# Linear attention feeding a bilinear FFN: narrow column tiles for the first two batches, batch 1 woven into the FFN, kv by chunk

## The chip, the cores and the metric

The kernel runs on one core of one Trainium2 chip. The metric is device time in microseconds (us), the median of several executions. The time of the kernel before was 353.69 us (three runs, 353.16 to 354.46). The span in a profile is about 2 us shorter than the device time of the same run. Engines are named as in the profile: PE (matrix multiply), PEld (its weight loads), DVE (VectorE), ACT (ScalarE), POOL (GpSimd, here a DMA issuer), SP (SyncE, here the second DMA issuer).

## The reference

```python
# q, k, v: (8 batches, 8 heads, 576 tokens, 64) float32; g_norm: (64,)
kv  = np.einsum('bhsd,bhse->bhde', k, v)            # 64 x 64 per head
out = np.einsum('bhsd,bhde->bhse', q, kv)
rms = np.sqrt(np.mean(out * out, axis=-1, keepdims=True) + 1e-06)
x   = (out / rms * g_norm)                          # -> (4608 tokens, 512)
y   = ((x @ w_a) * (x @ w_b)) @ w_out               # 512 -> 1536 -> 512
```

The attention part has no softmax. A whole batch must be reduced into kv before one of its tokens can be finished.

## The kernel before

The FFN works in nine strips of 512 tokens. A strip has 12 columns `fc` (eight 512-column matmuls each, `a` and `b`), and four output groups of 12 matmuls. While strip s runs, the attention of batch s+1 is woven into it: one call of `step` after each column or group (each such place is a *slot*). Strip 0 needs batch 0, so batch 0 comes first, alone, and batch 1 runs alone between strip 0 and strip 1. These two take the "early" path: q is transposed on PE, because the DMA transposition through scratch memory would be too late (batch 2's landed only at 62.4 us).

```python
# early path, batches 0 and 1: reorder on DVE, so that two heads lie side by side (128 columns)
def early_in(self, hs):
    for n in ("k", "q"):
        nc.vector.tensor_copy(t[n + "r"][:, :, hs, :],
                              t[n][:, hs, :, :].rearrange("p h c d -> p c h d"))
def qT(self, p, ...):
    for c in range(EC):                                        # 6 chunks of 96 tokens
        nc.tensor.transpose(ps[:, c*EP:(c+1)*EP], self.t["qr"][:, c, hs, :], ident[0:EP, 0:EP])
    ... copy to qs ...
def kv(self, p, ...):                                          # both paths
    rows = [EP] * EC if self.early else [128] * NCH + [SB]     # late: 128,128,128,128,64
    for c, r in enumerate(rows):
        nc.tensor.matmul(self.kv_ps[i][:, p, :], lhsT=self.k[0:r, c, hs, :],
                         rhs=self.v[0:r, hs, c, :], start=(c == 0), stop=(c == len(rows)-1))

# per head pair p and half h of the tokens, all batches
def xu(self, p, h):   # x = kv^T q on PE;  sq = x*x on ACT
def ss(self, p, h):   # sum of squares on PE; rs = 1/sqrt on ACT; xt = x*g*rs on DVE

def slices(self):                       # the ten steps of a batch from 2 on
    for p in range(NP):                 # four pairs of heads
        self.kv(p)
    self.kv_out(0, NP); yield
    ... eight steps of xu and the ss of the half before, and a last ss ...

dummies(24)
...batch 0...; columns 0 to 11 of strip 0; dummies(4); ...batch 1, in two halves...   # cut
for s in range(1, N_STRIP):
    nxt = s + 1 if s + 1 < B else None
    if nxt:
        load_qT(loaded[nxt])            # transposing DMA on the SP queue
        ...
    o_at = [4, 6, 8, 10] if s == 1 else [2, 5, 8, 11]
    t_at, s_at = (7, 9) if s == 1 else (0, 2)      # slots: reorder of k, first step
    ...
```

`dummies(n)` are n matmuls on zeros, whose only use is to keep PE active.

## Time and profile before

| what | value | view |
|---|---|---|
| time, span | 353.69 us, 352.1 us | times, page |
| PE busy | 332.4 us (94%) | page, part 1 |
| 512-column matmul, start to start | 0.216 us; 1296 of them are 280 us | single starts in the trace |
| batch 0, to strip 0's third column | 25.65 us | timeline |
| batch 1 alone | 42.7 to 60.98 us | timeline, windows |
| strip 1 | 60.98 to 98.62 us | timeline, windows |
| kv of a later batch | 1.94 us for 20 matmuls (the prediction said 1.85, from the chain) | timeline |

The page of the kernel before. The rows of digits are 40 slices of the span, each digit a busy share in tenths; PEclk is the clock that PE was granted.

```profile
span 352.1 us, 4345 instructions
...
PE 332.4 (94%) x1643; PEld 157.9 (45%) x1674; DVE 134.7 (38%) x229; ACT 134.2 (38%) x276; POOL 59.6 (17%) x71
...
PE   8689956999989999999999999999999999999995
...
PEclk9679976999989999999999999999999999999999
...
PE 90%; DVE 3%; ACT 2%; DMA 2%; issue 2%; POOL 0%; ACTq 0%; DVEq 0%; POOLq 0%
```

PE is the bound, as the chain of waits (last line) says too. What is left to win is where the PE row is below 9 or the clock row is below 9: near the start, around slices 5 and 6, counted from 0 (batch 1), and in slice 11 (end of strip 1).

The windows view of the kernel before, for the last ten columns of strip 0, for batch 1, and for strip 1:

```profile
core 0: us, PE busy (x) PEld busy (x) DVE busy (x) ACT busy (x) POOL busy (x), PEclk, DMA share, GB/s
25.65:42.70 17.05, 17.00 (x78) 7.70 (x79) 7.50 (x11) 6.16 (x11) 10.12 (x11) 1.00 1.32 202
42.70:60.98 18.28, 11.84 (x74) 5.83 (x75) 8.64 (x16) 8.18 (x20) 9.66 (x8) 0.75 1.71 177
60.98:98.62 37.64, 36.09 (x179) 17.00 (x181) 14.10 (x23) 15.09 (x32) 6.39 (x6) 0.98 1.33 141
```

Batch 1 alone holds PE busy for 11.84 of 18.28 us, at three quarters of the clock, and partly with zeros. The timeline (start, duration, engine, line, what; in brackets the idle time before it and its releaser) shows how it begins:

```profile
42.92 1.03 PE L172 MATMUL w_ps<-zt 128*128 128x512 bf16 x4
...
43.80 1.51 DVE L220 COPY kr_t<-k_t 96x1536 bf16<-96x1536 bf16 x1
45.23 0.54 DVE L220 COPY eqr_98<-eq_97 96x1536 bf16<-96x1536 bf16 x1
...
45.82 0.68 PE L235 MATMUL q_ps<-ident,eqr_98 96*128 96x96 bf16 x12 [1.88 <-DVE eqr_98 L220]
```

Transposes wait for the two reorder copies. Then the timeline of PE for one later kv group, and for the end of strip 1:

```profile
176.01 2.01 PE L202 MATMUL kv_ps<-v_t,kr_t 128*128 128x128 bf16 x20
```

```profile
97.05 0.28 PE L258 MATMUL s_ps<-sq,ones 128*128 128x288 bf16 x1 [0.70 <-ACT rs L260]
97.60 0.28 PE L244 MATMUL x_ps<-qT,kvd_123 128*128 128x288 bf16 x1 [0.27 <-DVE xt_155 L262]
...
98.48 0.30 PE L258 MATMUL s_ps<-sq,ones 128*128 128x288 bf16 x1 [0.28 <-DVE xt_155 L262]
...
99.92 0.59 PE L307 MATMUL a_ps<-xt_156,wa_t 128*128 128x512 bf16 x1 [0.49 <-DVE xt_156 L262]
```

Seven slots were left for ten steps, so three run bare at the end of the strip. The matmul of 0.59 us in the last line already runs at half clock (0.38 at full clock).

### The profile page before, as it was taken

To read this page: it belongs to the slowest core of one execution; us is meant where nothing else is said; L and a number is where in the kernel's file an instruction comes from. 1 tells how busy PE (TensorE), PEld (TensorE's weight loads), DVE (VectorE), ACT (ScalarE), POOL (GpSimd) and SP (SyncE) were. 2 spreads that over 40 slices of the span, in tenths; PEclk is the share of its full clock that TensorE was granted. 3 is DMA by queue.
4 is the path that set the end of the run, shared out by engine and by line. 5 is a ranking of instruction groups with operands and counts; after the bars stand their busy time and mean duration, and the time that the engine had idled before them with its cause. 6 is when DMAs were issued, how large, how long until landed. Compare 5 with 4: busy or idle time off the path is not lost.

```text
span 352.1 us, 4345 instructions
## 1 busy us (share of the span) xinstructions
PE 332.4 (94%) x1643; PEld 157.9 (45%) x1674; DVE 134.7 (38%) x229; ACT 134.2 (38%) x276; POOL 59.6 (17%) x71
## 2 busy tenths in 40 slices
PE   8689956999989999999999999999999999999995
PEld 3444423445435444544454445444544444444442
DVE  2544453342442453245334533453344232332310
ACT  1543344313643643364336433643464212223211
POOL 8746527006015001500110000000000000000000
PEclk9679976999989999999999999999999999999999
DMA  7999999989939913990591040004001000011022
GB/s 106 197 196 200 206 180 167 181 78 142 150 69 136 125 32 75 151 134 30 81 171 41 30 98 31 30 33 95 33 30 30 32 31 31 30 53 39 30 61 89
DMA packets 78981, 32.14 MB, mean 91 GB/s; under 512 B 49776, under 2 KB 74352, under 8 KB 78960
## 3 DMA queue, kind: packets, MB, share of 16 engines
q0 software_dynamic: 59408, 18.88, 49.6%
q1 hardware_dynamic: 19552, 12.98, 14.3%
q8 instruction: 13, 0.21, 0.3%
q14 instruction: 8, 0.07, 0.0%
HBM read 37.75 MB, written 12.98 MB: 144 GB/s over the span
## 4 chain that ended last, share of the span: by engine, by line
PE 90%; DVE 3%; ACT 2%; DMA 2%; issue 2%; POOL 0%; ACTq 0%; DVEq 0%; POOLq 0%
PE a_ps L307 27%; PE o_ps L332 26%; PE b_ps L307 26%; PE kv_ps L202 4%; PE s_ps L258 3%; PE x_ps L244 2%; DMA v_t<-in_v_dram 2%; ACT rs L260 2%; PE q_ps L235 1%; DVE kr_t L220 1%; DVE xt_156 L262 0%; ACT sq L252 0%; DVE xt_153 L262 0%; DVE xt_155 L262 0%; DVE xt_154 L262 0%
## 5 line engine op out<-in xcount | busy, mean ns | idle before, releaser
L319 DVE TENSOR_TENSOR abt<-b_ps,a_sb 128x512 bf16<-128x512 f32 x108 | 74.6, 692 | 117.1 <-PE b_ps L307 112.5
L332 PE MATMUL o_ps<-wo_t,abt 128*128 128x512 bf16 x419 | 97.7, 379 | 0.6
L317 ACT CAST a_sb<-a_ps 128x512 bf16<-128x512 f32 x108 | 63.3, 587 | 91.1 <-PE a_ps L307 89.7
L307 PEld LDWEIGHTS <-wb_t 128*128 128x128 bf16 x432 | 42.5, 98 | 53.5 <-issue 3.8
L332 PEld LDWEIGHTS <-abt 128*128 128x128 bf16 x432 | 41.8, 98 | 48.0
L307 PEld LDWEIGHTS <-wa_t 128*128 128x128 bf16 x432 | 42.7, 99 | 45.8 <-issue 2.5
L307 PE MATMUL a_ps<-xt_156,wa_t 128*128 128x512 bf16 x108 | 41.1, 381 | 1.6 <-DVE xt_156 L262 1.6
L307 PE MATMUL b_ps<-xt_153,wb_t 128*128 128x512 bf16 x108 | 41.7, 386 | 0.2 <-issue 0.2
L307 PE MATMUL a_ps<-xt_155,wa_t 128*128 128x512 bf16 x108 | 41.2, 382 | 0.3
L307 PE MATMUL b_ps<-xt_155,wb_t 128*128 128x512 bf16 x108 | 41.2, 381 | 0.2
L307 PE MATMUL a_ps<-xt_153,wa_t 128*128 128x512 bf16 x106 | 40.9, 386 | 0.3
L307 PE MATMUL b_ps<-xt_154,wb_t 128*128 128x512 bf16 x105 | 40.0, 381 | 0.0
L307 PE MATMUL a_ps<-xt_154,wa_t 128*128 128x512 bf16 x103 | 39.5, 384 | 0.2 <-issue 0.2
L307 PE MATMUL b_ps<-xt_156,wb_t 128*128 128x512 bf16 x101 | 38.5, 381 | 0.0
L252 ACT ACTIVATE sq<-x_ps 128x288 bf16<-128x288 f32 x64 | 25.9, 411 | 31.7 <-PE x_ps L244 31.6
L260 ACT ACTIVATE rs<-s_ps,eps_t 128x288 f32<-128x288 f32 x64 | 31.9, 498 | 14.6 <-PE s_ps L258 14.2
L343 DVE COPY o_sb<-o_ps 128x512 f32<-128x512 f32 x18 | 12.4, 692 | 45.4 <-PE o_ps L332 45.4
L341 ACT COPY o_sb<-o_ps 128x512 f32<-128x512 f32 x18 | 10.6, 586 | 49.4 <-PE o_ps L332 46.5
L258 PE MATMUL s_ps<-sq,ones 128*128 128x288 bf16 x64 | 19.8, 310 | 4.3 <-ACT rs L260 1.9
L66 POOL DMA_DIRECT2D k_t<-in_k_dram x6 | 5.4, 896 | 91.7 <-DVE kr_t L179 86.7
L146 POOL DMA_DIRECT2D scr<-in_q_dram x12 | 19.6, 1640 | 6.2 <-DMA wo_t<-in_moe_w_out_dram 5.3
L202 PE MATMUL kv_ps<-v_t,kr_t 128*128 128x128 bf16 (+2 forms) x168 | 16.6, 231 | 0.3 <-DMA v_t<-in_v_dram 0.2
(68 smaller groups left out, 158.4 us busy)
## 6 DMA issues: line engine op xcount, KB each, us to landing
out_dram<-o_sb SPq DMA_DIRECT2D x24, 256.0 KB, 2.0
scr<-in_q_dram POOLq DMA_DIRECT2D x12, 288.0 KB, 12.3
k_t<-in_k_dram POOLq DMA_DIRECT2D x6, 512.0 KB, 7.5
v_t<-in_v_dram POOLq DMA_DIRECT2D x6, 512.0 KB, 8.0
wa_t<-in_moe_w_a_dram POOLq DMA_DIRECT2D x6, 256.0 KB, 9.2
wb_t<-in_moe_w_b_dram POOLq DMA_DIRECT2D x6, 256.0 KB, 10.1
wo_t<-in_moe_w_out_dram POOLq DMA_DIRECT2D x2, 768.0 KB, 14.8
out_dram<-o_sb SPq DMA_DIRECT2D x12, 128.0 KB, 2.4
```

Source lines behind the costliest of these rows:

```text
L146: nc.gpsimd.dma_start(out=scr[:, :, hl, :].rearrange("p s d -> s p d"), in_=qv[hl])
L202: nc.tensor.matmul(self.kv_ps[i][:, p, :], lhsT=self.k[0:r, c, hs, :], rhs=self.v[0:r, hs, c, :], start=(c == 0), stop=(c == len(rows) - 1),)
L244: nc.tensor.matmul(ps, lhsT=self.kvd[:, p, :], rhs=self.q[p][:, h * HF : (h + 1) * HF], start=True, stop=True,)
L252: nc.scalar.activation(sq, ps, AF.Square)
L258: nc.tensor.matmul(ps, lhsT=ones, rhs=self.sq[p, h], start=True, stop=True)
L260: nc.scalar.activation(rs, ps, AF.Abs_reciprocal_sqrt, bias=eps_t)
L307: nc.tensor.matmul(getattr(self, which), lhsT=w[:, kc, self.fc * 128 : (self.fc + 1) * 128], rhs=xt[kc][:, t0 : t0 + STRIP], start=(kc == ...
L317: nc.scalar.copy(a_sb, self.a)
L319: nc.vector.tensor_mul(t, self.b, a_sb)
L332: nc.tensor.matmul(o_ps, lhsT=ab[s, fc][:, g * 128 : (g + 1) * 128], rhs=wo_t[:, fc, :], start=(fc == 0), stop=(fc == FC - 1),)
L341: nc.scalar.copy(o_sb, o_ps)
L343: nc.vector.tensor_copy(o_sb, o_ps)
```

## The change

Its intent: drop the reorder copies by working on one head at a time (64 columns of the array each, two heads in two column tiles); load batch 0 by pair of heads with q first; weave batch 1 into the last two columns of strip 0 and into three output groups, each cut in half over its 12 matmuls; order the later kv by chunk; start batch 2 earlier in strip 1. The first 256 columns of `w_a` and `w_b` are also loaded in two pieces instead of one, and the first two columns of strip 0 are ordered anew. The core of the diff:

```diff
-        def early_in(self, hs): ...                      # the DVE reorder copies are gone
+        def early_kv(self, p, pool):
+            ps = pool.tile([128, D], FP32, name="kv_ps", tag=tags[pool])
+            for hl in range(2):
+                for c in range(EC):
+                    nc.tensor.matmul(ps[hl * D : (hl + 1) * D, :],
+                        lhsT=t["k"][:, 2 * p + hl, c, :], rhs=t["v"][:, 2 * p + hl, c, :],
+                        start=(c == 0), stop=(c == EC - 1))
+        def early_qT(self, p, pool, act=False):           # same, 12 transposes 96x64
...
+        def kv(self):                                     # batches 2 to 7
+            for c in range(NCH + 1):
+                r = 128 if c < NCH else SB
+                for p in range(NP):
+                    nc.tensor.matmul(ps[:, p, :], lhsT=self.k[0:r, c, hs, :], ...,
+                        start=(c == 0 and p == 0), stop=(c == NCH and p == NP - 1))
...
-    dummies(24)
+    dummies(22)
+    for p in range(NP):                                   # batch 0, pair by pair
+        if p == 0: at0.early_qT(0, fpsum)
+        at0.early_kv(p, fpsum)
+        ...
+        dummies(1)
+        at0.xu(p, 0); at0.xu(p, 1)
+        if p + 1 < NP: at0.early_qT(p + 1, fpsum)
+        ...
+    for fc in range(2, 10): ffn_ab(0, fc)
+    at1.early_qT(0, apsum); at1.early_qT(1, apsum, act=True)
+    ffn_ab(0, 10)
+    at1.early_kv(0, apsum); at1.early_kv(1, apsum)
+    ffn_ab(0, 11)
+    ... xu, ss, early_qT, early_kv of batch 1, with o_mm(0, g, range(0, 6)) for g = 0, 1, 2 between ...
+    for g in range(3):
+        o_mm(0, g, range(6, FC)); o_out(0, g)
...
-        o_at = [4, 6, 8, 10] if s == 1 else [2, 5, 8, 11]
-        t_at, s_at = (7, 9) if s == 1 else (0, 2)
+        o_at = {10: 3} if s == 1 else {2: 0, 5: 1, 8: 2, 11: 3}
+        t_at, s_at = (4, 5) if s == 1 else (0, 2)
...
-                        step(gen)
+                        step(gen, 2 if s == 1 and slot in (7, 10) else 1)
```

## The prediction

> **What bounds it now.** The tensor engine. The page has PE busy 332.4 of 352.1 us; the chain that ended last is 90% PE. In the timeline a 512-column matmul starts every 0.216 us when dense: 1296 FFN matmuls are a floor of 280 us. The rest:
>
> - Start to 25.6 us, batch 0. Timeline: transposes at 8.5, first x at 10.85, last xt at 24.6; the slice row shows the clock down to 0.6 around 11 to 21 us.
> - 42.7 to about 62 us, batch 1: 19 us almost without FFN work. A DVE reorder of k (1.51 us) and q, then the ACT/DVE chain per half (sq 0.41, rs 0.50, xt 0.52); windows give clock 0.76.
> - End of strip 1 (97 to 103.4 us): batch 2's last steps, not woven, leave gaps near 3 us; a half-clock window then costs about 1.7 us.
> - kv of batches 2 to 7: 1.85 us per 20 matmuls. Single starts: 0.056 us between 128-row chunks, but 0.151 into and 0.159 out of the 64-row chunk, four times a batch.
> - 3.6 us tail, unchanged.
>
> **What the change does**
>
> 1. kv by chunk: one visit to 64 rows instead of four. Three visits x 0.2 us x 6 batches: **-3.6 us**, all on PE, which is critical. The Trainium skill, "TensorEngine Tiling (Array Packing)", Key Properties, says that changing tiling mode drains the engine; the trace agrees (about 0.2 us a visit).
> 2. Batch 0: loads by pair, q first, no DVE reorder copies. First x at about 9.4 us; then about 3.1 us a pair (sq, sq, rs, rs, xt, kv copies in series), 3.5 if the clock drops; strip 0's third FFN column starts at about 23.8 instead of 25.65: **-1.8 us** (0 to -3).
>    Added: twice as many transposes and kv matmuls, each with 64 columns. "TensorE: Matmul & The Clock Gate", section LDWEIGHTS, gives columns/1.2 ns, 53 ns for 64; so I estimate 55 to 60 ns each, 0.65 to 0.7 us per 12, against 0.043 and 0.056 each before with half as many. No run shows it yet. Plus mode switches.
> 3. Batch 1 woven: from its first transpose to strip 1 there are now two FFN columns (3.45 us) and three output groups (7.8 us). PE work is about 18.3 us, with switches about 20. Exposed about 9 us instead of 19: **-10 us** (-7 to -12).
> 4. Strip 1: batch 2 starts at slot 5, with two double steps, so all ten steps end inside the strip: **-4 us**. Against it: its transposed q is now issued behind output stores on the SP queue, landing near 68 us, just when wanted: up to +1.5.
>
> Sum about -19 us. From below: strip 1 at 57.6, plus 165.7 (columns), 85.5 (33 groups), 19.7 (six batches), 3.6, and 1 of stalls = 333 us span, 335 us on the device.
>
> **Prediction: 335 us, 8 in 10 within 330 to 341.** Faster by over 2%: 0.95; within: 0.04; slower: 0.01.
>
> **Right if**: kv groups take 1.25 to 1.3 us; no gap over 1 us nor cold window at the end of strip 1; strip 1 starts at 56 to 59 us; 64-column matmuls start 50 to 60 ns apart.
>
> **Wrong if**: 64-column weight loads do not overlap the matmuls (100 ns each would add 4 us per batch); the woven section goes to half clock; batch 2's transposed q or the second half of the output weights (landing near 47 us) comes late; or batch 0 runs cold, over 4 us a pair, giving back step 2.

## The result, and the profile after

The changed kernel took 339.11 us (median of four runs: 339.70, 335.17, 339.81, 338.52) against 354.02 us of the kernel before in the same rounds. The ratio is 0.956, with a 95% interval of 0.948 to 0.964. A ratio here is always the mean time of one kernel's fast runs over that of the other's of the same rounds, so it is not quite the ratio of the medians.

The four runs are spread over more than the kernel before ever was. Their mean granted clocks are 0.978, 1.000, 0.985 and 0.983, in the same order: the run at full clock is the fastest, but the other three are not in the order of their clocks. The profiled execution is the 339.70 us one. Its page:

```profile
span 337.8 us, 4546 instructions
...
PE 326.7 (97%) x1762; PEld 155.6 (46%) x1762; DVE 129.7 (38%) x223; ACT 133.0 (39%) x278; POOL 62.9 (19%) x76
...
PE   8899999978999999999999999999999999999995
...
PEclk9769999989999999999999999999999999999999
...
PE 91%; DMA 4%; ACT 2%; DVE 2%; issue 0%; SPq 0%; ACTq 0%; DVEq 0%
PE o_ps L321 28%; PE b_ps L293 26%; PE a_ps L293 26%; DMA qT<-scr 4%; PE x_ps L232 3%; PE s_ps L246 3%; PE w_ps L169 2%; PE kv_ps L220 2%; ACT rs L248 1%; PE q_ps L204 1%; PE kv_ps L190 0%; ACT sq L240 0%; DVE xt_155 L250 0%; DVE xt_154 L250 0%; SPq L350 0%
```

The hole of batch 1 is gone. A new one stands in slice 8, the clock dips with it, and a DMA that the chain did not hold before, the transposition of q (`qT<-scr`), now makes up 4% of the chain. Windows for columns 2 to 9 of strip 0, for the woven section, and for strip 1:

```profile
core 0: us, PE busy (x) PEld busy (x) DVE busy (x) ACT busy (x) POOL busy (x), PEclk, DMA share, GB/s
25.15:39.05 13.90, 13.90 (x64) 6.13 (x63) 6.11 (x9) 5.13 (x9) 9.20 (x10) 1.00 1.36 200
39.05:57.12 18.07, 17.31 (x166) 9.16 (x166) 8.37 (x18) 10.02 (x25) 7.97 (x8) 1.00 1.63 191
57.12:88.99 31.87, 28.47 (x146) 13.62 (x144) 12.71 (x21) 14.17 (x30) 9.64 (x8) 0.95 1.70 176
```

The section from 39.05 to 57.12 us holds two columns and three groups of FFN work as well as batch 1, at full clock. Timeline of PE there, and then in strip 1:

```profile
39.05 0.81 PE L204 MATMUL q_ps<-ident,eq_94 96*64 96x96 bf16 x24
...
41.63 0.66 PE L190 MATMUL kv_ps<-v_t,k_t 96*64 96x64 bf16 x24
```

```profile
67.47 1.38 PE L220 MATMUL kv_ps<-v_t,kr_t 128*128 128x128 bf16 x20
...
70.31 0.38 PE L293 MATMUL b_ps<-xt_157,wb_t 128*128 128x512 bf16 x1
72.97 0.28 PE L232 MATMUL x_ps<-qT,kvd_122 128*128 128x288 bf16 x1 [2.28 <-DMA qT<-scr]
```

The kv group of 20 fell from 1.94 to 1.32 us (first start to the next matmul's start). The last line is the new hole: batch 2's first x waits 2.28 us for its transposed q. The SP queue shows why it is late:

```profile
55.45 3.42 SPq L350 DMA_DIRECT2D out_dram<-o_sb  x6
59.00 6.04 SPq L155 DMA_TRANSPOSE qT<-scr  x1
```

The transposition is issued only after the six stores of the three groups that moved ahead of strip 1. It landed at 72.9 us. In the kernel before, it was issued at 50.7 and landed at 62.4.

Where the span went, stage by stage (starts read from the timeline; the three groups that moved are 3 x 2.59 = 7.77 us, so they are added to the earlier stage and taken from strip 1 for the kernel before):

| stage | before | changed, profiled first | changed, profiled in the first series below |
|---|---|---|---|
| start to strip 0's third column | 25.65 | 25.15 | 22.72 |
| to strip 1, with three groups of strip 0 | 43.10 | 31.97 | 31.97 |
| strip 1, with one group | 29.87 | 31.87 | 29.91 |
| strips 2 to 8 and tail | 253.49 | 248.81 | 248.81 |
| span | 352.1 | 337.8 | 333.4 |

### The profile page after: what moved, and what is told of

Its sections match the earlier page's. It is cut to its first block, busy times and chain, and to the rows that moved or that the text cites. A ratio compares the mean times of both kernels' runs of the same rounds, so it can differ in the third digit from the quotient of the medians.

```text
span 337.8 us, 4546 instructions
## 1 busy us (share of the span) xinstructions
PE 326.7 (97%) x1762; PEld 155.6 (46%) x1762; DVE 129.7 (38%) x223; ACT 133.0 (39%) x278; POOL 62.9 (19%) x76
## 4 chain that ended last, share of the span: by engine, by line
PE 91%; DMA 4%; ACT 2%; DVE 2%; issue 0%; SPq 0%; ACTq 0%; DVEq 0%
PE o_ps L321 28%; PE b_ps L293 26%; PE a_ps L293 26%; DMA qT<-scr 4%; PE x_ps L232 3%; PE s_ps L246 3%; PE w_ps L169 2%; PE kv_ps L220 2%; ACT rs L248 1%; PE q_ps L204 1%; PE kv_ps L190 0%; ACT sq L240 0%; DVE xt_155 L250 0%; DVE xt_154 L250 0%; SPq L350 0%
## 5 line engine op out<-in xcount | busy, mean ns | idle before, releaser
L321 PE MATMUL o_ps<-wo_t,abt 128*128 128x512 bf16 x432 | 98.7, 379 | 0.0
L293 PE MATMUL b_ps<-xt_156,wb_t 128*128 128x512 bf16 x108 | 41.4, 384 | 0.0
L293 PE MATMUL b_ps<-xt_155,wb_t 128*128 128x512 bf16 x108 | 41.4, 384 | 0.0
L293 PE MATMUL a_ps<-xt_154,wa_t 128*128 128x512 bf16 x108 | 41.4, 383 | 0.0
L293 PE MATMUL a_ps<-xt_157,wa_t 128*128 128x512 bf16 x108 | 40.9, 379 | 0.5 <-DVE xt_157 L250 0.5
L293 PE MATMUL b_ps<-xt_154,wb_t 128*128 128x512 bf16 x108 | 41.4, 383 | 0.0
L293 PE MATMUL a_ps<-xt_155,wa_t 128*128 128x512 bf16 x108 | 41.2, 381 | 0.0
L293 PE MATMUL a_ps<-xt_156,wa_t 128*128 128x512 bf16 x108 | 41.2, 381 | 0.0
L293 PE MATMUL b_ps<-xt_157,wb_t 128*128 128x512 bf16 x108 | 41.2, 381 | 0.0
L143 POOL DMA_DIRECT2D scr<-in_q_dram x12 | 19.6, 1640 | 10.2 <-DMA wo_t<-in_moe_w_out_dram 5.5
L246 PE MATMUL s_ps<-sq,ones 128*128 128x288 bf16 x64 | 18.9, 305 | 1.5 <-ACT rs L248 1.5
L250 DVE SCALAR_TENSOR_TENSOR xt_155<-x_ps,g_col,rs 128x288 bf16<-128x288 f32 x16 | 8.2, 517 | 15.4 <-ACT rs L248 15.3
```

The lines of the kernel that those rows point to most:

```text
L143: nc.gpsimd.dma_start(out=scr[:, :, hl, :].rearrange("p s d -> s p d"), in_=qv[hl])
L246: nc.tensor.matmul(ps, lhsT=ones, rhs=self.sq[p, h], start=True, stop=True)
L250: nc.vector.scalar_tensor_tensor(out=xt[p][:, t0 : t0 + HF], in0=self.x_ps[p, h], scalar=g_col, in1=rs, op0=ALU.mult, op1=ALU.mult,)
L293: nc.tensor.matmul(getattr(self, which), lhsT=w[:, kc, self.fc * 128 : (self.fc + 1) * 128], rhs=xt[kc][:, t0 : t0 + STRIP], start=(kc == ...
L321: nc.tensor.matmul(o_ps[s, g], lhsT=ab[s, fc][:, g * 128 : (g + 1) * 128], rhs=wo_t[:, fc, :], start=(fc == 0), stop=(fc == FC - 1),)
```

## The experiments

Eleven of the twelve runs were timed in five rounds, in three series, each on one chip; one was a single look. Two profiled executions fell into a state where all matmuls were several times slower (see under `warm_batch0` and `qt_ahead`); the quoted medians count every run, the ratios only the fast ones. A profile is called *warm* here when batch 0 ran at full clock and *cold* when a half-clock stretch fell into it; *fillers* are the `dummies`.

### First series: is it the clock, the queue, the weaving, the kv order?

**`after_again`**: the changed kernel, no edit.

> The changed kernel once more, as the control of this series. Its four runs so far were 335.2, 338.5, 339.7 and 339.8 us with mean granted clocks of 1.000, 0.983, 0.978 and 0.985. Theory (the half-clock windows in batch 0 and after the stall in strip 1 make the spread): times follow the clock, about 335 us where it stays 1.0 and 338 to 340 us where it is near 0.98. Rival (another cause): times do not order with the clock.

Measured: 335.77 us (335.41 to 336.44), clocks 0.995 to 1.000, ratio 0.951 (0.949 to 0.953). The profile has no half-clock stretch until the end:

```profile
PEclk9999999999999999999999999999999999999999
```

Runs at 0.995 to 1.000 took 335 to 336.5 us and runs at 0.978 to 0.985 took 338.5 to 340 us, on both chips, as the theory says; within each group the clock does not order the times. The two profiles of the same kernel differ by 4.4 us: 2.4 us in batch 0 (third column at 22.72 instead of 25.15), and 2.0 us in strip 1, where x waited 1.65 us instead of 2.44 and no half clock followed. (Waits of this kind, here and below, are the time between two starts less the matmul's normal interval. The bracket in the profile reckons from the modelled end and is a little smaller.)

**`qt_early`**: the transposed q of batch 2 goes on the queue before the stores.

```diff
+    load_qT(loaded[2])
     for g in range(3):
         o_mm(0, g, range(6, FC))
...
         if nxt:
-            load_qT(loaded[nxt])
+            if nxt > 2:
+                load_qT(loaded[nxt])
```

> Changed kernel with one edit: the transposing load of batch 2's q is put on the SP queue before the output stores of strip 0's first three groups instead of after them. In the changed kernel it was issued at 59.0 us, landed at 72.9 and left PE idle for 2.44 us, with a half-clock window after it. Theory A (it is late because of its place in the queue): issued near 52 us, when the scratch copy of q has landed (51.9), lands by 66, no gap before the first x of batch 2; about 2.4 us faster, up to 4 with the clock: 335 to 336.5 us. Rival B (it is late because the DMA engines are full, 1.6 of one engine's share in that stretch): it lands at 70 or later whatever the place, and the time stays within 1 us of the changed kernel.

Measured: 334.37 us (333.85 to 336.05), ratio 0.947 (0.945 to 0.949), 1.4 us less than the control of the same series. Queue and PE in its profile:

```profile
52.59 6.09 SPq L155 DMA_TRANSPOSE qT<-scr  x1
58.73 3.33 SPq L350 DMA_DIRECT2D out_dram<-o_sb  x6
```

```profile
70.50 0.29 PE L232 MATMUL x_ps<-qT,kvd 128*128 128x288 bf16 x1
```

It landed at 64.3 us, and the first x carries no wait. So the place in the queue was the cause, as theory A says; it landed before 66 us although the DMA engines were as full as before (DMA share between issue and landing 1.70, and 1.67 in the control). Of the 5.4 us by which it landed earlier than in the control's profile, 4.0 are the earlier issue and 1.4 a shorter transfer. The gain was below the 2.4 us that I expected, because the control of this series waited only 1.65 us. Strip 1 took 28.26 us instead of 29.91.

**`unwoven`**: batch 1 alone again, with everything else of the change kept.

```diff
+    ffn_ab(0, 10)
+    ffn_ab(0, 11)
     at1.early_qT(0, apsum)
     at1.early_qT(1, apsum, act=True)
-    ffn_ab(0, 10)
     at1.early_kv(0, apsum)
     at1.early_kv(1, apsum)
-    ffn_ab(0, 11)
...
-    o_mm(0, 0, range(0, 6))            # and the same for groups 1 and 2
...
-        o_mm(0, g, range(6, FC))
+        o_mm(0, g, range(FC))
```

> Changed kernel with batch 1 no longer woven: strip 0's last two columns run before it, its chain runs alone, the three output groups run whole after it. Column tiles, loads and all else as in the changed kernel. Theory (weaving is the largest part of the gain): the changed kernel needs 18.2 us from the first transpose of batch 1 to strip 1, of which 11.3 us is FFN work; alone, the chain of 16 sq and rs pairs (0.91 us each half) and the first copies should take 11 to 13 us, so 4 to 6 us slower than the changed kernel, up to 8 if the clock drops: 342 to 346 us. Rival (what helped in batch 1 is the loss of the reorder copies and the column tiles, weaving little): within 2 us of the changed kernel.

Measured: 340.37 us (339.75 to 341.78), ratio 0.964 (0.961 to 0.966): 4.6 us slower than the control, inside the 4 to 6 us. The windows view of its batch 1 alone:

```profile
42.44:52.00 9.56, 7.41 (x113) 4.09 (x114) 5.44 (x13) 7.75 (x21) 4.15 (x3) 0.90 1.75 186
```

This splits the gain of the batch 1 stage. Batch 1 alone took 18.28 us in the kernel before and 9.6 us here, without the reorder copies, with narrow matmuls and a tighter order. Half clock from 50.1 to 56.9 us followed in this profile and stretched the output groups by about 2 us. In all, from strip 0's third column to strip 1 with three groups, it took 37.0 us here, against 43.1 in the kernel before and 32.0 in the changed one: 6.1 us came without weaving, 5.0 with it. I had argued as if weaving were nearly all of it. Of the 6.1 us, PE's waits for the reorder copies were 2.04 and 0.40 us in the kernel before; no run splits the rest between narrow matmuls, order and dropped zeros, and no run tried the copies at an earlier place, though the k and q of batch 1's first half had landed by 33.4 us. About 0.9 of the 5.0 us is given back in strip 1 (28.98 us here, 29.91 woven), because without weaving x waited 0.72 us for batch 2's q instead of 1.65.

**`kv_chunk_only`**: the kernel before, with only the new kv order of batches 2 to 7 (the loop over chunks outside, over pairs inside, one start flag for the bank, as in the change).

> Kernel before with only the kv order of batches 2 to 7 changed: by chunk over all pairs. Theory: the group of 20 matmuls falls from 1.94 to 1.32 us in each of six batches, all of it on the critical engine: 3.7 us less, ratio 0.990 (350.2 us). Rival (the engine's time is given back in waits on the kv copies and x that follow): less than 1.5 us.

Measured: 349.64 us (348.58 to 349.89) against 353.62, ratio 0.9885 (0.987 to 0.991). 4.0 us less, against 3.7 expected. One group in its timeline:

```profile
139.16 1.38 PE L285 MATMUL kv_ps<-v_t,kr_t 128*128 128x128 bf16 x20
```

Nothing was given back: strips 3 to 6, which hold no half clock in either profile, took 34.37 us each instead of 34.99. This part of the change is pure PE time on the critical path.

### Second series: the clock in batch 0, the end of strip 1, a candidate

**`after_3`**: the changed kernel, as control.

> The changed kernel, as the control of this series. On the first chip three of four runs had clocks of 0.978 to 0.985 and took 338.5 to 339.8 us; on the second, five runs with clocks of 0.995 to 1.0 took 335.4 to 336.4 us. Which of the two this chip gives is not foretold; the time should go with the clock, 335 to 336 us at 1.0 and 337 to 340 us at 0.98.

Measured: 335.82 us (334.16 to 339.81; the last was counted as slow). Clocks 0.993 to 1.000, and 0.978 for the one of 339.81. Again the run with the lowest clock is the longest; but runs at 0.994 and 0.993 took 337.26 and 335.73 us, so the mean clock alone does not set the time. In this third profile of the changed kernel x waited 2.01 us for batch 2's q and no half clock followed; after the waits of 2.44 us (first profile) and 2.49 us (`one_column`) it did.

**`warm_batch0`**: more fillers in batch 0.

```diff
-        dummies(1)
+        dummies(3)
         at0.xu(p, 0)
```

> Changed kernel with three fillers instead of one before the first x of each pair of batch 0. The waits for the kv copy there were 0.69 us (pair 0) and 1.24 us (pair 1) from the start of the filler, so 0.65 us of fillers fit at full clock. Theory (the low activity of the 3.4 us window around 9 to 12.6 us, busy share 0.38 by my count, brings the half clock): the clock stays at 1.0 through batch 0 in every run, strip 0's third column starts at 22.6 to 23.2 us in the profile (25.15 in the changed kernel's cold run, 22.9 in its warm one); where the control's runs are cold, 2 us faster; where they are warm, within 0.5 us. Rival (the clock falls for another reason, such as narrow matmuls and transposes not counting as activity): still half clock in some runs, no gain.

Measured: 336.77 us (four runs of 335.76 to 337.36, and one of 1921.88), ratio 0.951 (0.948 to 0.953), clocks 0.993 to 1.000 in the four good runs. Its profiled execution was the one of 1921.88 us: every 512-column matmul started 1.28 us after the one before instead of 0.216, from beginning to end, with no clock record in the trace. That run told nothing about the theory, so it was repeated (`warm_again`, below).

**`strip1_only`**: the kernel before, with batch 2 started earlier in strip 1.

```diff
-        t_at, s_at = (7, 9) if s == 1 else (0, 2)
+        t_at, s_at = (5, 6) if s == 1 else (0, 2)
```

> Kernel before with only the place of batch 2's steps in strip 1 changed: reorder after slot 5 instead of 7, steps from slot 6 instead of 9, so that ten slots hold the ten steps and none is left for the end. Theory (the rushed end of strip 1 cost about 3.1 us of gaps and 1.7 us of half clock): 4 to 5 us faster, ratio 0.986 to 0.989, no half-clock window near 100 us. Rival (the waits only move: transposed q, k or v of batch 2, which landed at 62.4, 53.7 and 58.2 us, or ACT's chain, hold the earlier steps): under 2 us.

Measured: 350.81 us (350.18 to 351.26) against 353.85, ratio 0.991 (0.989 to 0.993): 3.0 us faster, between the two theories. The half clock at 100 us is gone, and so are the bare steps; what stays is a wait of the new strip for the last xt, which comes with having the last step in the last slot:

```profile
98.87 0.38 PE L307 MATMUL a_ps<-xt,wa_t 128*128 128x512 bf16 x1 [0.51 <-DVE xt L262]
```

Strip 1 took 35.93 us instead of 37.64, and the rest 251.94 instead of 253.49. So the repair of the end of strip 1 was worth 3.0 us in all, not 4 to 5.

**`best`**: a candidate from the changed kernel, with `qt_early`, three fillers, and batch 2 from slot 4.

```diff
-        t_at, s_at = (4, 5) if s == 1 else (0, 2)
+        t_at, s_at = (3, 4) if s == 1 else (0, 2)
...
-                        step(gen, 2 if s == 1 and slot in (7, 10) else 1)
+                        step(gen, 2 if s == 1 and slot == 9 else 1)
```

> A candidate that should beat both: the changed kernel with the early issue of batch 2's transposed q, three fillers in batch 0, and batch 2's steps in strip 1 from slot 4 (reorder after slot 3) with one double step instead of two. The early issue alone gave 1.4 us, fillers 0 to 2 by the clock, one double step less about 0.8. Expected 332.5 to 334 us, with little spread. Rival: the transposed q, which landed at 64.3 us with the early issue, is again just too late for the earlier start, and the gain of the steps is lost: 334 to 335 us.

Measured: 338.88 us (334.93 to 340.86; the four runs that counted as fast lie from 334.93 to 339.49), ratio 0.953 (0.949 to 0.958). A miss: 3 us slower than the control by the medians (0.953 against 0.948 by the fast runs, where the intervals just overlap), though strip 1 itself took only 27.46 us. The loss came one strip later: strip 2 took 38.88 us, and 35.03 in the changed kernel. The queue and PE, from its profile:

```profile
81.59 6.21 SPq L155 DMA_TRANSPOSE qT<-scr  x1
```

```profile
93.91 0.28 PE L232 MATMUL x_ps<-qT,kvd 128*128 128x288 bf16 x1 [2.00 <-DMA qT<-scr]
```

That is batch 3's transposed q. The program issues it at the start of strip 2. Strip 2 now starts at 82 us instead of 85 to 89, while the loads of later batches still fill the DMA engines (a scratch copy of q landed at 92.9), so it took 12.3 us from issue to landing; in the first profile of the changed kernel it took 4.5, issued at 88.6. Half clock followed from 94.7 to 98.1 us, and batch 4's q was late by 1.08 us as well. The data itself had been in scratch memory since 67.8 us: the wait was made by the place of the issue.

### Third series: issue ahead

**`qt_ahead`**: the changed kernel, transposed q issued one strip ahead for all batches.

```diff
+    load_qT(loaded[2])                      # before the stores, as in qt_early
...
         if nxt:
-            load_qT(loaded[nxt])
...
+                    if slot == 6 and nxt + 1 < B:
+                        load_qT(loaded[nxt + 1])
```

> Changed kernel, only the issue of the transposed q moved: batch 2's ahead of strip 0's output stores (as in qt_early), and those of batches 3 to 7 in the middle of the strip before the one that uses them (after slot 6) instead of at the start of the strip itself. In the candidate that started batch 2 earlier, batch 3's load was issued at 81.6 and landed at 93.9 us, 2.16 us after PE wanted it, and batch 4's was 1.08 us late. Theory (those waits are only issue time): no wait of PE for qT over 0.2 us anywhere; here, where strip 1 is not shortened further, the gain over the changed kernel is that of qt_early, 1.4 us, 334 to 335 us. Rival (the DMA engines are the limit): waits for qT stay.

Measured: 334.27 us (five runs of 333.21 to 336.05, median 333.92, and one of 866.87), ratio 0.945 (0.942 to 0.948). The time is what the theory says. The profiled execution was the one of 866.87 us, in which 512-column matmuls started 0.62 us apart throughout, so whether all waits for qT are gone cannot be read here; `best2` shows it.

**`best2`**: `best` with the issue ahead.

> The candidate with those waits taken out: transposed q ahead for all batches, three fillers in batch 0, batch 2 from slot 4 with one double step. The first candidate's profile had 2.16 + 1.08 us of waits for qT and 1.7 us of half clock after them, in a run of 337.5 us. Theory: without them 332.5 to 333.5 us, spread under 1.5 us. Rival: other work takes up the wait and it stays above 334.5.

Measured: 332.77 us (332.11 to 333.16) against 353.90, ratio 0.940 (0.937 to 0.943). Clock 0.999 to 1.000 in all five runs. Correct. Timeline of the SP queue and the first x of batch 2:

```profile
51.79 5.90 SPq L155 DMA_TRANSPOSE qT<-scr  x1
57.74 3.33 SPq L350 DMA_DIRECT2D out_dram<-o_sb  x6
...
67.42 6.39 SPq L155 DMA_TRANSPOSE qT<-scr  x1
```

```profile
66.42 0.29 PE L232 MATMUL x_ps<-qT,kvd 128*128 128x288 bf16 x1
```

Batch 3's q is issued at 67.4 and landed at 80.0, 12 us before it is used; no x waits for it. After 24 us the profile holds four waits over 0.25 us (0.60, 0.50, 0.87, 0.67), all on the ACT and DVE chain. This version beats both kernels; the third series has no run of the changed kernel, so this rests on the ratios to the kernel before, 0.940 here and 0.948 to 0.956 there, whose intervals do not overlap. Its spread is 1.1 us, on one chip; that of the changed kernel was 4.6, 1.0 and 5.7 us on three, so a smaller spread is not shown.

**`warm_again`**: the same kernel as `warm_batch0`.

> warm_batch0 once more, since its profiled execution was one in which every matmul ran about six times slower (1922 us) and told nothing. Theory: the profile shows clock 1.0 from the end of the first fillers to the last pair of batch 0, third column of strip 0 at 22.5 to 23.2 us; no run below clock 0.99 from batch 0. Against the changed kernel's warm runs no gain (335 to 337 us).

Measured: 336.29 us (336.10 to 336.92), ratio 0.951 (0.948 to 0.954), clocks 0.998 to 1.000. The clock row of its profile:

```profile
PEclk9999999999999999999999999999999999999999
```

The third column of strip 0 starts at 22.77 us; it was 22.72 in the warm profile of the changed kernel and 25.15 in the cold one. Of six profiles of kernels with one filler and a readable clock (the changed kernel three times, `qt_early`, `unwoven`, `one_column`), five have half clock inside batch 0, for 3.4 to 10.2 us; of three with three fillers (`best`, `best2`, `warm_again`), none. So far the fillers do what they were meant to do. Against a warm run there is nothing to win in batch 0, and the time did not fall; this profile is even 1.6 us longer than the one of `after_again` (335.0 against 333.4), because x waited 2.08 us for batch 2's q instead of 1.65, and 1.12 us for batch 4's. What the fillers are worth together with the earlier issue is not shown: no run adds them to `qt_ahead` alone.

**`one_column`**: both heads of a pair in one column tile.

```diff
-            ps = pool.tile([128, D], FP32, name="kv_ps", tag=tags[pool])
+            ps = pool.tile([128, 2, D], FP32, name="kv_ps", tag=tags[pool])
...
-                        ps[hl * D : (hl + 1) * D, :],
+                        ps[0:D, hl, :],
...
-            nc.vector.tensor_copy(self.kvd[D:, p, D:], ps[D:, :])
+            nc.vector.tensor_copy(self.kvd[D:, p, D:], ps[0:D, 1, :])
```

> Changed kernel, the kv matmuls of batches 0 and 1 of both heads of a pair in the same column tile (both write PSUM partitions 0 to 63, in two halves of the free side; the copy moves head 1 to partitions 64 to 127). In the changed kernel 12 such matmuls took 0.27 us from first start to last, starts of the two heads falling 5 and 27 ns apart by turns. Theory (the two column tiles run at the same time): here 12 starts in a row 32 ns apart and about 0.4 us in all. Rival (the matmuls are simply short, and the array takes one at a time): still 0.27 us. The kernel's time should not move by more than 1 us either way.

Measured: correct, one run of 339.48 us at clock 0.983. Twelve kv matmuls started 0.032 us apart, 0.37 us from the first to the last, against 0.27 us in the changed kernel. Two pairs in batch 1:

```profile
40.73 0.94 PE L190 MATMUL kv_ps<-v_t,k_t 96*64 96x64 bf16 x24
```

The same line took 0.66 us in the changed kernel (shown above). So the two column tiles do run at the same time. The kernel's time says nothing here: one run, with half clock in it, and no control on that chip.

## Why the prediction was right or wrong

The range (330 to 341 us) held the time, and the mechanisms named were the ones that acted. Two terms of the sum were mis-sized, and one mechanism was right but under-rated. Of the prediction's own tests, one "wrong if" case did occur: batch 2's transposed q came late. Of its "right if" list, the narrow matmuls did not start 50 to 60 ns apart, the kv group took 1.32 us and not 1.25 to 1.3, and strip 1 began between 56 and 59 us in the first profile (57.12) but not in the second (54.69). That the number fitted so well is partly luck: the second profile's span, 333.4 us, is almost the 333 that was summed up from below, because strip 1 began 2.9 us earlier and the rest took 3.2 us longer than predicted.

| step of the prediction | predicted | shown |
|---|---|---|
| 1, kv by chunk | -3.6 us | six times 1.94 less 1.32 is -3.8; alone -4.0 (`kv_chunk_only`). Right |
| 2, batch 0 | -1.8 (0 to -3) | -0.5 where the clock halved, as it did in the kernel before; -2.9 where it did not, so most of that is the clock. Inside the range, but two-valued |
| 3, batch 1 woven | -10 (-7 to -12) | -11.1 (43.10 to 31.97). Right in size, but less than half of it is weaving |
| 4, strip 1 | -4, and up to +1.5 against it | +1.1 in the first profile, -0.9 in the second (strip 1 without its kv gain, with the 1.6 us of half clock that followed it before). Mis-sized |

For step 4 the sum is: before, 29.87 us + 1.57 us of half clock after the strip - 0.63 us of kv gain = 30.81; changed, 31.87 or 29.91. The transposed q was named as the thing that could come late, with a landing near 68 us and up to 1.5 us. It landed at 72.9 and 69.7 us and cost 2.44 and 1.65 us. In the first profile half clock followed as well, which I had not counted as its consequence. A landing near 68 us would be an issue near 56.5 us and the 11.7 us to landing of the kernel before; it was 59.0 and 13.9 in the first profile, 56.6 and 13.1 in the second. Why the same transfer takes 1.4 to 2.2 us longer there is open (`qt_early`, issued earlier, had 11.7 again). `qt_early` shows that another place in the queue is enough to take the whole wait away. The other side of the step, the -4 us, was too large as well: `strip1_only` measured 3.0.

The cost of the narrow matmuls was wrong in the good direction. I worked out 55 to 60 ns each, 0.65 to 0.7 us per 12, from the Trainium skill, "TensorE: Matmul & The Clock Gate", section LDWEIGHTS (columns / 1.2, 53 ns for 64). Measured: 12 transposes in 0.35 us and 12 kv matmuls in 0.27 us from first start to last, against 0.21 and 0.28 us for the six wide ones of before (0.043 and 0.056 us each). I missed two things. In one column tile the starts are 32 ns apart, so loads of 53 ns one after another do not set the pace. And the two heads' tiles overlap, as the skill's "TensorEngine Tiling (Array Packing)", Key Properties, says of tiles in general (different tiles can load and multiply in parallel); the starts of the two heads fall 5 and 27 ns apart by turns, and `one_column` takes the overlap away. The mode switches that I added, without a figure for one, are in the trace: about 0.09 us before and 0.1 us after each narrow group.

The clock: the prediction named a cold batch 0 as a risk. The profiles fit an activity window in part. The trace's half-clock stretches, but for the last one of each run, are multiples of 3.41 us, which is the window that "TensorE: Matmul & The Clock Gate", Part 1, describes as free-running against the start of the kernel. In the first profile such a window began at 9.2 us; at 0.216 us for 512 columns, its matmuls fill 44% of it (the 0.38 in the expectation of `warm_batch0` is not what this count gives), and half clock followed. In the warm one the windows lay 0.6 us later relative to the program, with 51% and more, and no half clock followed. But the count gives no threshold: half clock followed a window of 46% (`unwoven`, from 9.1 us) and did not follow windows of 43% (`kv_chunk_only`, from 95.4 us) and 39% (`warm_again`, from 67.9 us). None of the three profiles with three fillers has half clock in batch 0. That the phase of the window decides between 335 and 339 us is argued from these profiles; no run sets the phase, so it is not shown.

From below, the prediction had strip 1 starting at 57.6 us and 275.5 us from there on. The first profile had 57.12 and 280.7; what it has more is the wait for q (2.44), the half clock after it (about 1.5) and three waits on the ACT and DVE chain in strip 1 and at its end (0.74, 0.87, 0.67), of which the prediction had allowed 1 us. The second had 54.69 and 278.7.

## What to carry to other kernels

When work is moved ahead, look at what stood behind it in a shared in-order queue: here three output groups moved forward, and their stores held a prefetch back until 4.3 to 7.1 us after its source had landed (three profiles of the changed kernel), which cost most or all of what the earlier start of the next batch had won. Issue prefetches when their source is ready, not where the consumer begins; a stage that is shortened otherwise meets the same wait one stage later (`best` was no faster than the control, `best2` with the issue ahead the fastest of all). And count the visits to a different tile shape: regrouping 20 matmuls so that the short chunk comes once instead of four times took a third off their time, at no cost that `kv_chunk_only` shows.

## What the Trainium skill lacked or had wrong

- "TensorE: Matmul & The Clock Gate", LDWEIGHTS: columns / 1.2 ns (53 ns for 64 columns) is given as the time of one load; read as the pace of alternating loads and matmuls, as the prediction did, it is too slow. 64-column loads with 64-column matmuls start 32 ns apart in `one_column`. The profile of the kernel before could have warned of it: its 128-column pairs start 56 ns apart, where the formula gives 107. "TensorEngine Tiling (Array Packing)", Restrictions, says that column tiling disables the fast weight load; if it does, it did not show as a much slower pace here (32 ns for 64 columns, 56 for 128).
- "TensorE: Matmul & The Clock Gate", Part 3, says that matmuls start in program order. With two column tiles the trace of the changed kernel has kv matmuls of head 0 starting before the last transposes of head 1, which come earlier in the program (timeline of PE):

```profile
8.29 0.47 PE L204 MATMUL q_ps<-ident,eq_91 96*64 96x96 bf16 x10
8.57 0.23 PE L190 MATMUL kv_ps<-v_t,k_t 96*64 96x64 bf16 x2
8.60 0.21 PE L204 MATMUL q_ps<-ident,eq_91 96*64 96x96 bf16 x1
8.63 0.20 PE L190 MATMUL kv_ps<-v_t,k_t 96*64 96x64 bf16 x1
8.64 0.21 PE L204 MATMUL q_ps<-ident,eq_91 96*64 96x96 bf16 x1
```

- "TensorEngine Tiling (Array Packing)", Key Properties, says that changing the mode drains the engine, without a cost. Here a visit to a 64-row chunk among 128-row ones cost about 0.2 us (0.151 us to the first start and 0.159 us after it, instead of 0.056 each), and a visit to a column tile about 0.2 us as well.
- "TensorE: Matmul & The Clock Gate", caveats, mentions a clock stuck at a quarter for 50 us. Two executions here were slower throughout: 512-column matmuls 1.28 us apart over 1920 us, and 0.62 us apart over 865 us, instead of 0.216, with no clock record at all and a reported clock of 1.0.
